# Which weights and values stay in SBUF between two rounds of a four-layer decode kernel, and where the others are put

## The chip, the cores and the metric

The kernel runs on one core of one Trainium2 chip. The metric is the device time of one execution in microseconds (us). The kernel before was run three times: 173.87, 174.04 and 174.45 us, a median of 174.04 us.

## What is computed

One token for each of four sequences goes through four residual layers: attention, gated unit, attention, gated unit. Both attentions use the same `wq`, `wo`, key and value caches, and both gated units the same `w_gate`, `w_up`, `w_down`.

```python
# x: 4 x 1 x 512, wq: 512 x 4096, wo: 4096 x 512; 32 query heads, 8 key/value heads of 128
def _A_ref(x, k_cache, v_cache, wq, wo):          # attention over the last W = 2048 positions
    q = (x @ wq).reshape(B, Sq, Hq, Dh).transpose(0, 2, 1, 3)
    k = jnp.repeat(k_cache[:, :, Sk - W:, :], rep, axis=1)
    v = jnp.repeat(v_cache[:, :, Sk - W:, :], rep, axis=1)
    p = softmax(einsum("bhqd,bhkd->bhqk", q, k) * Dh ** -0.5)
    return einsum("bhqk,bhkd->bhqd", p, v).transpose(0, 2, 1, 3).reshape(B, Sq, Hq * Dh) @ wo

def _B_ref(x, w_gate, w_up, w_down):              # 512 -> 1792 -> 512
    h = sigmoid(x @ w_gate) * (x @ w_up)
    return h @ w_down

x = x + _A_ref(layernorm(x), ...)
x = x + _B_ref(layernorm(x), ...)
x = x + _A_ref(layernorm(x), ...)
x = x + _B_ref(layernorm(x), ...)
```

All inputs are bf16. Keys and values of the window are 16 MiB each, `wq` and `wo` 4 MiB each, the three weights of the gated unit 1.75 MiB each.

## The kernel before: a plan of places, and one queue of loads

**Units.** SBUF places are counted in units: 256 bf16 columns on 128 partitions, 64 KiB. A head's keys or values (`V0_h` in the first attention, `V2_h` in the second) take 32 units, half of `wq` 32, one row block of `w_gate` or `w_up` 7 (`g0` to `g3`, `u0` to `u3`; two adjoining ones are loaded in one transfer of 14), and one of the 14 row blocks of `w_down` 2 (`d4` to `d6` is written `d4`, by its first block).

**Places.** `kt` holds all keys, transposed once in the first attention and read again in the second, where the values of later heads take the place of the keys that have been used. `wo_sb` (`ws` in the code) holds `wo`. `arena` (`ar`) has 75 units, `side` (`sx`) 31. `pt` holds softmax weights, `pb` the exponentials of the softmax, `qs` the queries. Between the attentions part of `wo_sb` (units 8 to 27) is copied to PSUM (`stash`, L1026, on VectorE at L1036) and copied back by ScalarE (L1031) at the start of the second attention, so that its place can take weights in between. The table `WHERE` (L430 and on) gives each tensor's place: buffer, first unit and length; `_1` or `_3` at the end of a name is the layer (first or second gated unit).

**What is kept.** Keys, `wo` and the second half of `wq` are read from HBM once. Of the values, the first attention leaves units 24 to 31 of head 0 in the arena (at 66) and units 19 to 31 of head 7 (at 23); `VKEEP` (L308) tells `load_v` (L471) to skip the load of these pieces in the second attention. Of the gated unit, `u01` and `g01` stay in the arena (`KEEPG`, L299; `load_g`, L1042). All else is loaded twice.

**Order.** All loads are issued by SyncE in one order, that of the program; a load waits, and with it all that come after it, until the instructions that read or wrote its place before are done. The other engines' instructions are ordered by a planner (`_schedule`) with fixed costs, and then run in that order, waiting on semaphores. The order of the loads from the end of the first attention on is: values of head 7 in two pieces, `u01`, `g01`, `g23`, `u23`, six pieces of `w_down`, the first half of `wq` in three pieces (`q01`), values of head 0 (24 units in four pieces) and head 1 (32 units in two), heads 2 to 7 into `kt`, `g23`, `u23`, four pieces of `w_down`.

**Instructions.** In the second attention a head goes through: scores (L763), their maximum and exponentials (L772 to L785), a turn (L791, L796), the weights (L821 on VectorE, L828 on ScalarE), the sums (L836), values (L921, or L863 and L879 where several heads' columns are packed), and `wo` (L961, L988). TensorE runs the score of a head two heads ahead of its values (`AHEAD`). The gated unit (`glu`, L1136) does `w_up` and `w_gate` at L1157 and `w_down` at L1233 in the first, at L1230 in the second. The queries of the second attention are made at L703, and the result of the second attention becomes the input of the last layer (`xn`) at L1071.

Of the kernel before, what the change touches and what calls it, by code (L numbers as in the profile page):

```python
# [268 lines left out]
def build(nc, A_x, A_k, A_v, A_wq, A_wo, B_wg, B_wu, B_wd, out):  # L269
# [4 lines left out]
    _, HKV, SK, DH = A_k.shape  # L274
# [24 lines left out]
    KEEPG = 4  # L299
# [8 lines left out]
    VKEEP = {0: 24, 7: 19}  # L308
# [30 lines left out]
    with es:  # L339
# [82 lines left out]
        G0 = MAIN - KEEPG * GU  # L422

# [7 lines left out]
        for n in range(HKV - 1):  # L431
            WHERE["V0_%d" % HEADS1[n]] = [ar(MAIN - UHEAD if n % 2 == 0 else 0, UHEAD)]
        WHERE["V0_%d" % (HKV - 1)] = [ar(0, 19), ar(23, 13)]
        WHERE["u01"], WHERE["g01"] = ar(52, 2 * GU), ar(38, 2 * GU)
        PT3 = ("kt", 187, 4)
        WHERE.update({
            "g23_1": ("ws", 8, 2 * GU), "u23_1": ar(0, 2 * GU),
            "d0_1": ar(14, 8), "d4_1": ("ws", 22, 6), "d7_1": ar(36, 2), "d8_1": ("qs", 0, 4), "d10_1": ("pb", 0, 4),
            "d12_1": ("pt", 4, 4),
            "q01": [("ws", 8, 10), ar(0, 14), ("ws", 18, 8)],  # L440
            "V2_0": [ar(14, 9), ar(36, 2), sx(0, 8), sx(8, 5), ar(66, 8)],
            "V2_1": [sx(13, NS - 13), ar(0, 14)],
            "V2_6": [("kt", 128, 16), ("kt", 144, 16)],
            "V2_7": [("kt", 160, 12), ("kt", 172, 7), ar(23, 13)],
            "g23_3": ar(0, 2 * GU), "u23_3": sx(0, 2 * GU),
            "d0_3": ar(14, 8), "d4_3": ("kt", 192, 8), "d8_3": ("kt", 200, 8), "d12_3": sx(14, 4),
# [595 lines left out]
        def load_g(L, nm, ktc, keep):  # L1042
            key = (nm, ktc // 2, 0 if keep or (nm, ktc // 2, 0) in gkeep else L)
            if key not in gkeep:
                s = WHERE["%s%d%d" % (nm, key[1] * 2, key[1] * 2 + 1) + ("_%d" % L if key[2] else "")]
                gkeep[key] = s
                dma("w%s%d_%d" % (nm, L, ktc), blk_ap(s), (wg_d if nm == "g" else wu_d)[:, key[1], :], w=blk_tok(s),
                    rate="bw_7k")
            s = gkeep[key]
            return (s[0], s[1] + ktc % 2 * GU, GU)  # L1050

        def load_d(L, fc0, fc1):
# [4 lines left out]
                w=blk_tok(s) + (("qs",), ("qs1",)) * (s[0] == "qs"), rate="bw_4k")  # L1057
# [78 lines left out]
        def glu(L, last_layer):  # L1136
# [10 lines left out]
            for nm, ktc in (("u", 0), ("u", 1), ("g", 0), ("g", 1), ("g", 2), ("g", 3), ("u", 2), ("u", 3)):  # L1147
                bank = GB if nm == "g" else UB
                keep = not last_layer and 2 * ktc + (nm == "u") < KEEPG
                s = load_g(L, nm, ktc, keep)  # L1150
# [64 lines left out]
            if not last_layer:  # L1215
                parts[1:] = [(4, 7), (7, 8), (8, 10), (10, 12), (12, 14)]
# [207 lines left out]
```

## Time and profile before

The profile is of another execution than the three timed ones.

| | us |
|---|---|
| timed runs | 173.87, 174.04, 174.45 |
| profiled execution, device time | 174.79 |
| its span, from the first to the last instruction | 173.0 |
| TensorE busy (matmul) | 136.2 |
| VectorE busy | 100.7 |
| ScalarE busy | 77.3 |
| HBM read | 68.62 MB, 397 GB/s over the span |
| mean granted TensorE clock | 0.822 |

The span runs from 0 to 173.0. The first attention takes it to about 105, the first gated unit to 119, the second attention to 162 and the last layer to the end. In the profile's slices a digit is the busy share in tenths of one fortieth of the span; in its timeline a row has a start, a duration, the engine, the line, what is written and read, a count of instructions, and in brackets the idle time of the engine before it with what ended that. A DMA row has the number of transfers, the size of each and the median time from issue to landing.

### The profile page before, as it was taken

What the parts mean: (1) busy time and instruction counts of PE and PEld (TensorE: products, weight loads), DVE (VectorE), ACT (ScalarE), POOL (GpSimd) and SP (SyncE); (2) the same over time, 40 slices, a digit from 0 to 9 for tenths busy, and PEclk for the clock granted to TensorE, in tenths of its full rate; (3) what the DMA queues carried; (4) which work ended last, traced back from release to release, by engine and by line L of the source; (5) the groups of instructions that cost most, each with busy time, mean ns of one, the idle gap of its engine ahead of it and who ended that gap; (6) DMA issues with size and microseconds to landing.
All of it is one profiled execution on the core that took longest, in us unless ns stands there. A gap on an engine that the chain in (4) does not pass through costs nothing.

```text
span 173.0 us, 4894 instructions
## 1 busy us (share of the span) xinstructions
PE 136.2 (79%) x2179; PEld 100.4 (58%) x2179; DVE 100.7 (58%) x252; ACT 77.3 (45%) x134; POOL 8.0 (5%) x19
## 2 busy tenths in 40 slices
PE   0395589899898779998979676657977989689883
PEld 0292388658466458565655366546625756458772
DVE  7535015886848675795797653113279877754450
ACT  2064207848576646566291230110767463554200
POOL 5200000000000000000000000202200000000020
PEclk9999756999999987999999755555569999956755
DMA  5999999999999999999999999999999999999960
GB/s 183 424 422 411 432 424 428 439 409 449 424 416 433 400 445 424 412 427 428 420 417 418 397 419 416 406 400 411 386 385 452 426 420 405 424 416 423 407 250 5
DMA packets 9361, 68.93 MB, mean 398 GB/s; under 512 B 1017, under 2 KB 1917, under 8 KB 6013
## 3 DMA queue, kind: packets, MB, share of 16 engines
q1 hardware_dynamic: 9332, 68.62, 95.7%
q8 instruction: 17, 0.28, 0.6%
q14 instruction: 4, 0.02, 0.0%
q10 hardware_dynamic: 8, 0.00, 0.0%
HBM read 68.62 MB, written 0.00 MB: 397 GB/s over the span
## 4 chain that ended last, share of the span: by engine, by line
DMA 65%; PE 23%; DVE 6%; ACT 2%; issue 2%; SPq 1%; DVEq 0%; ACTq 0%
DMA arena<-in_A_v_cache_dram 32%; DMA kt<-in_A_k_cache_dram 12%; DMA kt<-in_A_v_cache_dram 10%; DMA wo_sb<-in_B_w_down_dram 7%; PE ps L863 5%; PE ps L740 4%; DMA wo_sb<-in_A_wq_dram 4%; PE ps L763 3%; PE ps L1157 2%; PE ps L921 2%; SPq L464 1%; DVE pt L821 1%; PE ps L1230 1%; PE ps L836 1%; PE ps L988 1%
## 5 line engine op out<-in xcount | busy, mean ns | idle before, releaser
L750 ACT COPY kt<-ps 128x1024 bf16<-128x1024 bf16 x40 | 39.2, 1017 | 28.2 <-PE ps L740 28.0
L740 PE MATMUL ps<-ident_r,kt 128*128 128x128 bf16 x512 | 40.4, 238 | 5.1 <-DMA kt<-in_A_k_cache_dram 3.1
L740 PEld LDWEIGHTS ps<-ident_r,kt 128*128 128x128 bf16 x512 | 34.9, 109 | 11.8 <-issue 4.4
L750 DVE COPY kt<-ps 128x1024 bf16<-128x1024 bf16 x24 | 29.1, 1214 | 14.2 <-PE ps L740 14.0
L763 PE MATMUL ps<-kt,qs 128*32 128x512 bf16 x256 | 18.3, 413 | 1.2 <-ACT pb L785 1.2
L821 DVE TENSOR_TENSOR pt<-ps,ofbr 128x1024 bf16<-128x1024 f32 (+1 forms) x15 | 15.4, 1029 | 2.7 <-PE ps L796 2.7
L863 PE MATMUL ps<-arena,pt 128*64 128x512 bf16 (+1 forms) x128 | 13.1, 377 | 3.0 <-DMA arena<-in_A_v_cache_dram 3.0
L772 DVE TENSOR_REDUCE nmz<-ps 128x1 f32<-128x512 f32 x16 | 11.0, 688 | 5.9 <-PE ps L763 5.8
L791 DVE STREAM_TRANSPOSE pb<-pb 128x512 bf16<-128x512 bf16 x16 | 11.3, 704 | 4.2 <-ACT pb L785 4.1
L785 ACT ACTIVATE pb<-ps,nmz 128x512 bf16<-128x512 f32 x16 | 11.1, 692 | 5.8 <-DVE nmz L782 5.8
L828 ACT ACTIVATE pt<-ps,ofbr 128x96 bf16<-128x96 f32 x28 | 7.2, 342 | 7.8 <-PE ps L796 7.8
L863 PEld LDWEIGHTS ps<-arena,pt 128*64 128x64 bf16 (+1 forms) x128 | 5.9, 111 | 7.9 <-DMA arena<-in_A_v_cache_dram 4.0
L763 PEld LDWEIGHTS ps<-kt,qs 128*32 128x32 bf16 x256 | 5.8, 101 | 7.8 <-ACT pb L785 2.2
L872 ACT COPY arena<-ps 128x512 f32<-128x512 f32 (+1 forms) x7 | 3.9, 555 | 11.9 <-PE ps L863 11.7
L1031 ACT COPY wo_sb<-ps 128x1024 bf16<-128x1024 bf16 x5 | 5.0, 1011 | 9.1 <-PE ps L703 9.1
L836 PE MATMUL ps<-rowf,nmz 128*128 128x16 f32 x32 | 6.9, 292 | 2.7 <-DVE pt L821 2.5
L836 PEld LDWEIGHTS ps<-rowf,nmz 128*128 128x128 f32 x32 | 5.4, 212 | 5.8 <-DVE pt L821 4.2
L1157 PE MATMUL ps<-xn,arena 128*128 128x5 bf16 (+1 forms) x168 | 6.3, 172 | 2.2 <-DMA arena<-in_B_w_up_dram 1.1
L634 POOL TENSOR_TENSOR rs<-pt,rs 128x4 f32<-128x4 f32 x3 | 3.0, 1014 | 106.0 <-DVE pt L630 106.0
L879 PEld LDWEIGHTS ps<-arena 128*128 128x128 f32 x52 | 6.7, 201 | 2.1 <-ACT arena L872 1.6
L879 PE MATMUL ps<-arena 128*128 128x16 f32 x52 | 7.4, 273 | 0.6
L1157 PEld LDWEIGHTS ps<-xn,arena 128*128 128x128 bf16 x168 | 6.3, 118 | 2.5 <-DMA arena<-in_B_w_up_dram 1.2
(170 smaller groups left out, 162.9 us busy)
## 6 DMA issues: line engine op xcount, KB each, us to landing
kt<-in_A_k_cache_dram SPq DMA_DIRECT2D x8, 2048.0 KB, 24.6
arena<-in_A_v_cache_dram SPq DMA_DIRECT2D x7, 2048.0 KB, 20.2
kt<-in_A_v_cache_dram SPq DMA_DIRECT2D x3, 2048.0 KB, 14.9
wo_sb<-in_A_wo_dram SPq DMA_DIRECT2D x8, 512.0 KB, 25.1
kt<-in_A_v_cache_dram SPq DMA_DIRECT2D x4, 1024.0 KB, 19.3
kt<-in_A_wq_dram SPq DMA_DIRECT2D x1, 2048.0 KB, 11.7
side<-in_A_wq_dram SPq DMA_DIRECT2D x1, 1984.0 KB, 15.8
arena<-in_B_w_up_dram SPq DMA_DIRECT2D x2, 896.0 KB, 8.0
```

The costliest lines, as they stand in the source:

```text
L740: last = pe.transpose(bankb(bank)[:, (v * NB + q) * 128:(v * NB + q + 1) * 128], kt[:, c0:c0 + 128], ident_b[:, :])
L750: return (e.tensor_copy if ev == "vector" else e.copy)(to, fr)
L763: last = pe.matmul(ps[32 * b:32 * b + 32, sbk, 0:CB * 128], qs[:, q0:q0 + 32], blk_ap(kblk(h, b))[:, c * CB * 128:(c + 1) * CB * 128], sta ...
L772: lambda v: v.tensor_reduce(nmv, ps[:, sbk, 0:CB * 128], AXX, ALU.max, negate=True),
L785: o = a.activation(pbuf[:, :], ps[:, sbk, 0:CB * 128], ACTF.Exp, bias=gv, scale=1.0, accum_out=zv)
L791: P.op("vector", "ptr%d_%d" % (L, h), 650.0, lambda v: v.transpose(turned[:, :], pbuf[:, :]), r=[("pb", 0), ("pb", 1)], w=[("pb", 2), ("pb ...
L821: lambda v: v.tensor_tensor(pv4[:, 0:nj], spread(tbk, nj).unsqueeze(2).broadcast_to([128, nj, NB, REP]), ofb[:, :].unsqueeze(1).unsqueeze( ...
L828: last = a.mul(pv4[:, nj:NJ4, b, :], spread(MB, NJ4 - nj), ofb[:, b:b + 1])
L836: lambda pe: pe.matmul(ps[:, tbk, CB * NQ:CB * NQ + NR], zv.broadcast_to([128, 128]), rowf[:, :], start=True, stop=True),
L863: last = pe.matmul(ps[rows * g:rows * (g + 1), bank, 0:wide * 128].rearrange("p (c d) -> p c d", c=wide), ptv[:, w0:w0 + rows], v, start=( ...
L879: last = pe.matmul(ps[:, out[0], out[1]:out[1] + NR], part[:, c * 128:(c + 1) * 128], ey[wide][:, c * NR:(c + 1) * NR], start=(c == 0), st ...
L1157: last = pe.matmul(ps[:, bank, fc * wid:(fc + 1) * wid], cols[:, fc - g0, :], xn[:, ktc * (NB + 1):ktc * (NB + 1) + wid], start=(ktc == 0 ...
```

## The change

Other pieces stay, and nearly all transfers between the attentions get other places and a new order:

- **Values.** Head 0 keeps units 8 to 31 (24, at arena 50) instead of 24 to 31; head 7 keeps 17 to 31 (15, at arena 0) instead of 19 to 31.
- **Gate and up.** `u0`, `u1` and `g1` stay (21 units); `g0` is loaded again for the last layer, into `kt`.
- **First gated unit.** Loads come as `u01`, `g23`, `g01`, `u2`, `u3`; `u3` is in two pieces, in `pb` (4 units) and `qs` (3 units). TensorE takes the rows in the order `u0 u1 g2 g3 g0 g1 u2 u3`. `w_down` comes as `d4` (2 blocks), `d0` (4), `d8` (4), `d6` (2), `d12` (2) instead of `d0 d4 d7 d8 d10 d12`; `d0` and `d8` take the places of `g23` in `wo_sb`.
- **Queries of the second attention.** The first half of `wq` comes in four pieces of 10, 8, 10 and 4 units instead of 10, 14 and 8.
- **Second attention.** Before the loads into `kt` begin, 8 units of head 0 and 32 of head 1 are loaded.
- **Last layer.** `u01` and `g1` are there, then `g0`, `g23`, `u23` are loaded; its first `w_down` piece goes into `kt`.

The number of transfers is 63 for SyncE in both kernels. No arithmetic changes; sums over row blocks are taken in another order.

```diff
-    KEEPG = 4
+    KEPTG = {("u", 0), ("u", 1), ("g", 1)}
...
-    VKEEP = {0: 24, 7: 19}
+    VKEEP = {0: 8, 7: 17}
...
-        WHERE["V0_%d" % (HKV - 1)] = [ar(0, 19), ar(23, 13)]
-        WHERE["u01"], WHERE["g01"] = ar(52, 2 * GU), ar(38, 2 * GU)
+        WHERE["V0_%d" % (HKV - 1)] = [ar(15, 17), ar(0, 15)]
+        WHERE["u01"], WHERE["g01"] = ar(36, 2 * GU), ar(22, 2 * GU)
         PT3 = ("kt", 187, 4)
         WHERE.update({
-            "g23_1": ("ws", 8, 2 * GU), "u23_1": ar(0, 2 * GU),
-            "d0_1": ar(14, 8), "d4_1": ("ws", 22, 6), "d7_1": ar(36, 2), "d8_1": ("qs", 0, 4), "d10_1": ("pb", 0, 4),
-            "d12_1": ("pt", 4, 4),
-            "q01": [("ws", 8, 10), ar(0, 14), ("ws", 18, 8)],
-            "V2_0": [ar(14, 9), ar(36, 2), sx(0, 8), sx(8, 5), ar(66, 8)],
-            "V2_1": [sx(13, NS - 13), ar(0, 14)],
+            "g23_1": ("ws", 8, 2 * GU), "u2_1": ar(15, GU), "u3_1": ("pb", 0, 4), "u3_1b": ("qs", 0, 3),
+            "d4_1": ("ws", 24, 4), "d6_1": ("pt", 4, 4), "d0_1": ("ws", 8, 8), "d8_1": ("ws", 16, 8), "d12_1": ar(25, 4),
+            "q01": [ar(15, 10), ("ws", 8, 8), ("ws", 16, 10), ar(25, 4)],
+            "V2_0": [sx(0, 8), ar(50, 24)],
+            "V2_1": [sx(8, NS - 8), ar(15, 9)],
             "V2_6": [("kt", 128, 16), ("kt", 144, 16)],
-            "V2_7": [("kt", 160, 12), ("kt", 172, 7), ar(23, 13)],
-            "g23_3": ar(0, 2 * GU), "u23_3": sx(0, 2 * GU),
-            "d0_3": ar(14, 8), "d4_3": ("kt", 192, 8), "d8_3": ("kt", 200, 8), "d12_3": sx(14, 4),
+            "V2_7": [("kt", 160, 10), ("kt", 170, 7), ar(0, 15)],
+            "g0_3": ("kt", 0, GU), "g23_3": ar(15, 2 * GU), "u23_3": sx(0, 2 * GU),
+            "d0_3": ("kt", 8, 8), "d4_3": ("kt", 192, 8), "d8_3": ("kt", 200, 8), "d12_3": sx(14, 4),
         })
...
-            for nm, ktc in (("u", 0), ("u", 1), ("g", 0), ("g", 1), ("g", 2), ("g", 3), ("u", 2), ("u", 3)):
+            turn = [("u", 0), ("u", 1)] + [("g", a) for a in ((1, 0, 2, 3) if last_layer else (2, 3, 0, 1))] + [("u", 2), ("u", 3)]
+            for at, (nm, ktc) in enumerate(turn):
...
-                parts[1:] = [(4, 7), (7, 8), (8, 10), (10, 12), (12, 14)]
+                parts = [(4, 6), (0, 4), (8, 12), (6, 8), (12, 14)]
...
-        P.op("gpsimd", "qs_zero", 1200.0, lambda g: g.memset(qs[:], 0.0), w=[("qs",), ("qs1",)] + list(blk_tok(WHERE["d8_1"])))
+        P.op("gpsimd", "qs_zero", 1200.0, lambda g: g.memset(qs[:], 0.0), w=[("qs",), ("qs1",)] + list(blk_tok(WHERE["u3_1b"])))
```

The new `load_g` loads a row block by itself where `WHERE` names one, in two pieces if it names a second with a `b`, and otherwise the pair as before:

```python
        def load_g(L, nm, ktc):
            kept = (nm, ktc) in KEPTG
            name = "%s%d_%d" % (nm, ktc, L)
            if not kept and name in WHERE:
                got, f0 = [], 0
                for x in (name, name + "b"):
                    if x in WHERE:
                        s, c0 = WHERE[x], ktc % 2 * F + f0 * 128
                        dma("w" + x, blk_ap(s), (wg_d if nm == "g" else wu_d)[:, ktc // 2, c0:c0 + s[2] * UNIT], w=blk_tok(s) + qz(s),
                            rate="bw_4k")
                        got.append((s, f0))
                        f0 += 2 * s[2]
                return got
            key = "%s%d%d" % (nm, ktc // 2 * 2, ktc // 2 * 2 + 1) + ("" if ktc < 2 else "_%d" % L)
            s = WHERE[key]
            if key not in gkeep:
                gkeep[key] = s
                dma("w" + key, blk_ap(s), (wg_d if nm == "g" else wu_d)[:, ktc // 2, :], w=blk_tok(s), rate="bw_7k")
            return [((s[0], s[1] + ktc % 2 * GU, GU), 0)]
```

More of the change, by code (lines that the diff above doesn't have):

```diff
@@ L421, in build @@
         MAIN = WKEEP[2][0][1]
-        G0 = MAIN - KEEPG * GU
         def ar(u, n):
@@ L1040, in build, with qz @@
         gkeep = {}
-        def load_g(L, nm, ktc, keep):
-            key = (nm, ktc // 2, 0 if keep or (nm, ktc // 2, 0) in gkeep else L)
+        def qz(s):
+            return (("qs",), ("qs1",)) * (s[0] == "qs")
+        def load_g(L, nm, ktc):
[10 more added lines that the diff above has]
+                        f0 += 2 * s[2]
+                return got
+            key = "%s%d%d" % (nm, ktc // 2 * 2, ktc // 2 * 2 + 1) + ("" if ktc < 2 else "_%d" % L)
+            s = WHERE[key]
             if key not in gkeep:
-                s = WHERE["%s%d%d" % (nm, key[1] * 2, key[1] * 2 + 1) + ("_%d" % L if key[2] else "")]
                 gkeep[key] = s
[L1047 to L1050, printed above, removed]
+                dma("w" + key, blk_ap(s), (wg_d if nm == "g" else wu_d)[:, ktc // 2, :], w=blk_tok(s), rate="bw_7k")
+            return [((s[0], s[1] + ktc % 2 * GU, GU), 0)]
         def load_d(L, fc0, fc1):
@@ L1056, in load_d @@
             dma("wd%d_%d" % (L, fc0), blk_ap(s)[:, 0:(fc1 - fc0) * D], rows[:, (fc0 - g0) * D:(fc1 - g0) * D],
-                w=blk_tok(s) + (("qs",), ("qs1",)) * (s[0] == "qs"), rate="bw_4k")
+                w=blk_tok(s), rate="bw_4k")
             return s
@@ L1146, in glu, with e_g @@
             wid = NB if last_layer else NB + 1
-            for nm, ktc in (("u", 0), ("u", 1), ("g", 0), ("g", 1), ("g", 2), ("g", 3), ("u", 2), ("u", 3)):
+            turn = [("u", 0), ("u", 1)] + [("g", a) for a in ((1, 0, 2, 3) if last_layer else (2, 3, 0, 1))] + [("u", 2), ("u", 3)]
+            for at, (nm, ktc) in enumerate(turn):
                 bank = GB if nm == "g" else UB
-                keep = not last_layer and 2 * ktc + (nm == "u") < KEEPG
-                s = load_g(L, nm, ktc, keep)
-                def e_g(pe, ktc=ktc, s=s, bank=bank):
+                first, end = ktc == turn[0 if nm == "u" else 2][1], ktc == turn[-1 if nm == "u" else 5][1]
+                got = load_g(L, nm, ktc)
+                def e_g(pe, ktc=ktc, got=got, bank=bank, first=first, end=end):
                     last = None
@@ L1155, in e_g @@
                         g0, gn = WD[fc // 4]
-                        cols = blk_ap(s)[:, g0 * 128:(g0 + gn) * 128].rearrange("p (m j) -> p j m", j=gn)
+                        s, f0 = [x for x in got if x[1] <= fc][-1]
+                        cols = blk_ap(s)[:, (g0 - f0) * 128:(g0 - f0 + gn) * 128].rearrange("p (m j) -> p j m", j=gn)
                         last = pe.matmul(ps[:, bank, fc * wid:(fc + 1) * wid],
@@ L1159, in e_g @@
                                          xn[:, ktc * (NB + 1):ktc * (NB + 1) + wid],
-                                         start=(ktc == 0 and fc == 0), stop=(ktc == NC - 1),
-                                         skip_group_check=True)
+                                         start=(first and fc == 0), stop=end, skip_group_check=True)
                     return last
                 prev = [P.op("tensor", "glu_%s%d_%d" % (nm, L, ktc), 36.0 * NFC, e_g,
-                             r=list(blk_tok(s)) + [("xn",)], w=[("psg", bank, ktc)], banks=(bank,), order=prev)]
+                             r=[t for s, _ in got for t in blk_tok(s)] + [("xn",)], w=[("psg", bank, ktc)], banks=(bank,), order=prev)]
                 toks[nm].append(("psg", bank, ktc))
@@ L1233, in e_d @@
                                 last = pe.matmul(ps[:, YB, c * NB:(c + 1) * NB], wd, hf,
-                                                 start=(fc == 0 and c == 0), stop=(fc == NFC - 1),
+                                                 start=(fc == parts[0][0] and c == 0), stop=(fc == parts[-1][1] - 1),
                                                  skip_group_check=True)
```

## The prediction

> **What bounds the kernel now.** I read the slices of the profile first, then the DMA rows, then what TensorE waited for in the second attention, then its timeline.
>
> The slices (a digit per fortieth of the span, 4.3 us each):
>
> ```profile
> PEclk9999756999999987999999755555569999956755
> DMA  5999999999999999999999999999999999999960
> GB/s 183 424 422 411 432 424 428 439 409 449 424 416 433 400 445 424 412 427 428 420 417 418 397 419 416 406 400 411 386 385 452 426 420 405 424 416 423 407 250 5
> DMA packets 9361, 68.93 MB, mean 398 GB/s; under 512 B 1017, under 2 KB 1917, under 8 KB 6013
> ```
>
> The DMA engines are full from the first slice to the 38th, the passage between the attentions (slices 23 to 29) included. So fewer bytes are worth time, if the queue stays full and what follows the last loads can move up as well. Second, who waits at the end. The waits of TensorE between 126 and 163 us (total, times, longest):
>
> ```profile
> PE ps L863 <- DMA kt<-in_A_v_cache_dram: 1.6, 3, 0.9
> PE ps L836 <- DVE pt L821: 1.4, 2, 0.9
> PE ps L763 <- ACT pb L785: 1.2, 2, 0.7
> ```
>
> and its timeline there and in the last layer:
>
> ```profile
> 142.57 1.06 PE L863 MATMUL ps<-kt,pt 128*32 128x256 bf16 x32 [0.36 <-DMA kt<-in_A_v_cache_dram]
> ...
> 147.49 1.06 PE L863 MATMUL ps<-kt,pt 128*32 128x256 bf16 x32 [0.35 <-DMA kt<-in_A_v_cache_dram]
> ...
> 149.99 0.62 PE L863 MATMUL ps<-kt,pt 128*32 128x256 bf16 x16 [0.90 <-DMA kt<-in_A_v_cache_dram]
> ...
> 162.47 0.23 PE L1157 MATMUL ps<-xn,arena 128*128 128x4 bf16 x2 [0.28 <-DVE xn L1071]
> ...
> 170.03 0.53 PE L1230 MATMUL ps<-side,pt 128*25 128x128 bf16 x8
> ```
>
> The reader is to see that TensorE is nearly as long as the loads: of the 36 us from 126 to 162 it stands still for about 6, and for values only 0.36 + 0.35 + 0.90 = 1.6 us. After 162.47 it never waits for a load; the last load, 256 KB of `w_down` issued at 150.28 with 18.8 us to landing, is there at 169.05, 1.0 us before its matmuls at 170.03. So a byte saved is worth its transfer time to the loads, but only what TensorE has been waiting to the time.
>
> **Part 1: bytes.** Kept before: 8 + 13 units of values and 28 of gate and up, 49. After: 24 + 15 and 21, 60. So 11 units of 64 KiB, 0.72 MB, are not loaded. Heads 3 and 4 of the values, 32 units each, reach TensorE at 142.57 and 147.49, 4.92 us for 32 units: 0.154 us a unit. 11 units are 1.7 us. Where they are missing matters: heads 0 and 1 load 40 units instead of 56, so heads 2 to 6 land 16 x 0.154 = 2.5 us earlier; head 7 loads 17 instead of 19, so 18 units or 2.8 us for its last piece; `g0` (7) comes again, which leaves 1.7 us for everything after it. The last load should land at 169.05 - 1.7 = 167.35.
>
> **Part 2: the passage between the attentions.** 84 units stand between the values of head 7 and `wq` in both kernels (56 of gate and up, 28 of `w_down`), and 32 of `wq` behind, in the same number of transfers. The added waits are all on SyncE's queue, and behind each waits every later load. What a late issue costs needs the lead. The nearest row for a transfer into an empty queue is the output: 0.7 us of issue and 1.0 us of waiting for it, 1.7 us in all. Two rows of the passage:
>
> ```profile
> wo_sb<-in_A_wq_dram SPq DMA_DIRECT2D x1, 512.0 KB, 6.9
> side<-in_A_v_cache_dram SPq DMA_DIRECT2D x1, 512.0 KB, 6.7
> ```
>
> 512 KB need 8 x 0.16 + 1.7 = 3.0 us in an empty queue and took 6.7 at the least: the queue held nearly 4 us of work at its thinnest. A load that has to land at time T with u units does no harm if it is issued by T - 0.16 u - 1.7. Now each added wait, with landings from the rows of TensorE:
>
> ```profile
> 115.05 0.59 PE L1233 MATMUL ps<-pt,arena 128*128 128x4 bf16 x16 [1.54 <-DMA arena<-in_B_w_down_dram]
> ...
> 118.42 0.38 PE L1233 MATMUL ps<-pt 128*128 128x4 bf16 x8 [0.28 <-DMA pt<-in_B_w_down_dram]
> ```
>
> The first 8 units of `w_down` land at 115.0, all 28 at 118.4: 0.17 us a unit.
> - `u01` now covers the sums' place (arena 36, 37) and the identity at 40, which head 0's L879 reads until 100.4; before it was issued at 98.89. It landed 6.9 us later, at 105.8, so it may be issued until 105.8 - 2.2 - 1.7 = 101.9. Spare 1.5 us, cost 0.
> - `g01` waits for head 7's first piece, as `u23` did (issued 103.39); it has the place of `g23` in the queue, landing 110.2. Cost 0. `u3` waits for the turn of `pb` (L1014, done at 104.1): cost 0, `pb` lay in this queue before too.
> - `d0` goes where `g23` lay, so it waits for `g2`, `g3`. `g23` comes 14 units sooner, at 108.0, and TensorE is free for it after `u0`, `u1` at about 109.0 (`xn` first used at 107.39; 14 matmuls 0.5 to 0.6 us): issue at 110.1. As 12 of 28 units it has to land at 118.4 - 16 x 0.17 = 115.7, so by 112.7. Spare 2.6.
> - `wq`'s second piece goes where `d0` lay: 115.7 + 0.6 for 16 matmuls, issue at 116.3; it has to land 18 units after 118.4, at 121.3, so by 118.3. Spare 2.0. The third waits for `d8` (20 of 28 units, 117.0 + 0.6): 117.6 against 119.6. Spare 2.0. The fourth waits for `d12`, 118.8 against 121: spare 2.
> - The values of head 2 into `kt` still wait for the first scores, issued at 125.92. They landed 11.5 us later, at 137.5; now they are wanted at 135.0, so by 135.0 - 5.0 - 1.7 = 128.3. Spare 2.4 where it was 4.9. This is the stall that would be late next.
>
> Smaller rows (`u3` in 4 and 3 units) are about as many as go (pieces of 2 units), and 256 KB pieces follow each other at 0.7 us against 4 x 0.154: 0.1 us at most, either way; I take 0. The chain to the queries keeps its ends: `u3` lands at the 56th unit as `u23` did (112.4), `w_down` at 118.4, `wq` at 123.4; ScalarE's copies back start some 0.5 us later and are still ahead of the scores that need their banks. So I start the second attention at the same time.
>
> **Part 3: the second attention and the end.** With values 2.5 us earlier the three waits of 1.6 us go. VectorE is busy for 21.5 of the 26.5 us from 125.9 to 152.4, so it has room for this. The planner changes the order a little (head 4's scores come ahead of the turn of head 2's weights, the last head's scores later), so some of the 1.4 us at L836 and 1.2 us at L763 may grow; bounds 0 and the 1.6 won, I take 0.1. From `xn` to the end nothing waits for loads, before or after: `g23` and `u23` land 1.7 us earlier, the input 1.5. The bound by the loads is 170.03 - 167.35 = 2.7 us.
>
> **Sum.** 174.79 for the profiled execution, less 1.6, plus 0.1: 173.3 (span 171.5). The profiled execution stands 0.75 over the median of the runs; the same change on the median gives 174.04 - 1.5 = **172.5**.
>
> **Rivals.**
> 1. *More, up to the bound of the loads.* The clock:
>
> ```profile
> 148.87:152.28 3.41, 1.96 (x30) 1.46 (x30) 1.90 (x7) 1.52 (x6) 0.00 (x0) 1.00 1.02 425
> 152.28:159.10 6.82, 6.37 (x128) 4.84 (x129) 3.05 (x8) 3.19 (x9) 0.00 (x0) 0.50 1.00 411
> ```
>
> TensorE was busy for 1.96 of 3.41 us (first columns: window, length, TensorE), the 0.9 us wait among the rest, and then had half the clock for 6.8 us. At half the clock 16 matmuls of L863 took 1.07 for 0.62, L879 1.03 for 0.56, two groups of L988 0.60 for 0.39, L836 0.59 for 0.39: with the rest about 1.7 us. If the wait goes and the clock stays, 1.6 + 1.7 exceeds the bound of 2.7: 171.3. Against it: other short waits remain, and from 128.4 to 131.8 TensorE was as idle and kept its clock. The Trainium skill, "TensorE: Matmul & The Clock Gate", section "What's actually happening", says that the clock is halved after a free-running window of about 3.4 us with too little work; 6.8 us is two of these, and by that rule this rival would be the forecast.
> 2. *No change.* The loads are hidden: the waits for values turn into waits for VectorE, ScalarE or a reordered TensorE, and the start of the last layer stays at 162. For it: VectorE is busy for 3.33 of 3.42 us from 145.45 to 148.87. Against: it has idle time on both sides. 1.6 us won, 1.1 to 1.9 given back: 173.5 to 174.4, say 174.0.
> 3. *Slower: the ring of places runs dry.* `d0` waits for `g3`, `wq`'s second piece for `d0`, head 2's values for the queries from `wq`. If `d0`'s matmuls end more than 2.0 us after 116.3, every us more delays `wq`, the queries and so all of the second attention by one. To lose 0.7 net it takes 2.0 + 1.6 + 0.7 = 4.3 us: 174.7. Only a landing far off its place in the queue does that; against it speak the spares above.
> 4. *The load isn't skipped.* `load_v` skips where the kept piece begins at the unit in `VKEEP` (8, 17), which the new pieces do. I give this nothing of its own.
>
> **How the numbers follow.** Forecast (172.0 to 173.4) 0.58; rival 1 (171.0 to 172.0) 0.18; rival 2 0.15; rival 3 0.09. About 0.3% or 0.5 us is what a measurement of this kernel can tell from no change. Faster by that: 0.58 + 0.18 = 0.76; the same: rival 2, 0.15; slower 0.09. The range takes in the two neighbours, from the 171.3 of rival 1 to 174.1 in rival 2; it leaves out some 0.09 + 0.08.
>
> **What would show it.** HBM read 67.9 MB instead of 68.62. In the slices DMA stays at 9 through the passage. SyncE issues `wq`'s second piece near 116.3, head 2's values near 126. TensorE's waits for values of 1.6 us are gone, L1071 near 160.7 instead of 162.23, the last load at 167.3. Wrong would be a hole in DMA between 112 and 130 (rival 3), new waits of 1 us for L821 or L785 with L1071 at 162 (rival 2), or a full clock from 150 to 159 (rival 1).

## The result, and the profile after

The kernel after is slower: 175.17 us (median of 19 runs, 174.49 to 176.61) against 174.12 (19 runs, 173.38 to 174.6) for the kernel before in the same series. The ratio is 1.0068, with a 95% interval of 1.0052 to 1.0083. The forecast was 172.5, with a range of 171.3 to 174.1: a gain of 1.5 us was predicted (from 174.04), and a loss of 1.05 came.

The profiled execution of the kernel after took 176.61 us (span 174.8), the slowest of its runs, so it overstates the loss. A time read from a profile below is that of one execution. The slices after, to be held against those of before:

```profile
PEclk9999656999999999999999655555558699975555
DMA  5999999999999999999999999999989999999960
GB/s 181 420 436 426 420 424 420 431 411 446 420 424 427 404 432 435 415 430 412 435 425 402 396 332 406 387 352 353 358 346 410 429 424 411 420 417 416 410 262 6
HBM read 67.90 MB, written 0.00 MB: 389 GB/s over the span
```

The bytes are those that were predicted (67.90 MB). But the rate, which before was 385 to 452 GB/s in the passage (slices 23 to 32), is 332 in slice 24 and 346 to 358 in slices 27 to 30, and slice 30 has a DMA digit of 8. The windows of the passage in the kernel after, then in the kernel before (columns: window, length, busy TensorE, weight loads, VectorE, ScalarE, GpSimd, clock, DMA share, GB/s):

```profile
100.50:104.90 4.40, 3.38 (x58) 2.69 (x59) 2.41 (x6) 1.68 (x2) 0.00 (x0) 0.50 0.90 331
113.00:118.00 5.00, 1.96 (x53) 1.68 (x51) 0.51 (x3) 1.48 (x2) 0.97 (x1) 0.50 0.93 349
118.00:123.00 5.00, 4.23 (x127) 3.90 (x125) 1.94 (x11) 0.00 (x0) 0.50 (x2) 0.50 0.94 361
...
128.00:132.00 4.00, 3.22 (x30) 0.75 (x22) 2.56 (x9) 1.79 (x4) 0.00 (x0) 0.56 0.93 360
```

```profile
100.50:104.90 4.40, 3.52 (x82) 2.83 (x82) 1.94 (x7) 1.87 (x2) 0.00 (x0) 0.50 1.02 420
113.00:118.00 5.00, 2.34 (x64) 2.01 (x61) 0.51 (x3) 0.21 (x1) 0.42 (x1) 0.50 1.04 403
118.00:123.00 5.00, 4.34 (x131) 4.06 (x127) 1.94 (x11) 0.72 (x1) 1.75 (x3) 0.50 1.02 404
...
128.00:132.00 4.00, 2.29 (x32) 1.08 (x36) 3.62 (x9) 2.93 (x9) 0.00 (x0) 0.95 1.06 441
```

In the 14.4 us of the first three windows the kernel before moved 420 x 4.4 + 403 x 5 + 404 x 5 = 5883 KB, the kernel after 5006: 0.88 MB less, where the change saves 0.72 MB in all. The fourth window, in the first heads of the second attention, adds 0.32 MB. From 100 to 140 us the kernel after moved 15.02 MB, the kernel before 16.44; from there to the last loads it stays about as far behind. So it had lost 1.42 MB of transfers by then, twice what it saves, and its last load lands later (171.00 us) than before (169.05). A rate below that of before isn't by itself a loss of time: f4, the kernel before with its code shifted (below), moved 329 GB/s from 118 to 123 us and took no measurably longer. What TensorE waits for in the kernel after from the second attention's first scores to the end (total, times, longest; the first five rows):

```profile
PE ps L761 <- ACT pb L783: 1.2, 2, 0.7
PE ps L794 <- DVE pb L789: 1.0, 3, 0.4
PE ps L834 <- DVE pt L819: 0.9, 1, 0.9
PE ps L1170 <- issue: 0.9, 1, 0.9
PE ps L1242 <- issue: 0.5, 1, 0.5
```

The 1.6 us of waits for values (L863 before, L861 now) are gone, as predicted. New are 1.0 for the turn (L794) and 1.46 of "issue", where it was 0.76. The passage itself, in TensorE's timeline:

```profile
116.55 0.58 PE L1245 MATMUL ps<-pt,wo_sb 128*128 128x4 bf16 x16 [1.00 <-DMA wo_sb<-in_B_w_down_dram]
117.83 0.59 PE L1245 MATMUL ps<-pt,wo_sb 128*128 128x4 bf16 x16 [0.69 <-DMA wo_sb<-in_B_w_down_dram]
...
124.10 0.70 PE L701 MATMUL ps<-xn,wo_sb 128*128 128x4 bf16 x20 [0.68 <-DMA wo_sb<-in_A_wq_dram]
124.72 0.37 PE L701 MATMUL ps<-xn,arena 128*128 128x4 bf16 x8
125.57 2.75 PE L761 MATMUL ps<-kt,qs 128*32 128x512 bf16 x24 [0.48 <-DVE pt L714]
```

The last instruction that makes the input of the second attention (L560) starts at 119.59, the first scores at 125.57: 5.98 us. Before it was 118.83 (L562) and 123.98: 5.15.

A measure that recurs below: the distance from that input to the first scores (the passage), from the first scores to the first values in `kt`, from there to the input of the last layer (L1071 before, L1082 after), and from there to the end. Each row is one execution. The second and third distance trade against each other (g4, a form of the kernel before, has 16.83 and 21.30 in its profile), so a single one of them says little.

| profile | passage | to values in kt | to last layer | to the end | last load lands |
|---|---|---|---|---|---|
| before | 5.15 | 15.02 | 23.23 | 10.82 | 169.05 |
| after | 5.98 | 16.17 | 21.52 | 11.51 | 171.00 |
| after, g23 ahead (e3) | 5.95 | 15.49 | 21.29 | 11.54 | 169.70 |
| after, code shifted (f3) | 6.07 | 16.71 | 21.54 | 10.11 | 169.84 |

### The profile page after: what moved, and what is told of

Same layout as the page of the kernel before. It is cut to its first block, busy times and chain, and to the rows that moved or that the text cites. A ratio compares the mean times of both kernels' runs of the same rounds, so it can differ in the third digit from the quotient of the medians.

```text
span 174.8 us, 4895 instructions
## 1 busy us (share of the span) xinstructions
PE 135.9 (78%) x2179; PEld 99.3 (57%) x2179; DVE 100.8 (58%) x252; ACT 77.2 (44%) x134; POOL 8.0 (5%) x19
## 3 DMA queue, kind: packets, MB, share of 16 engines
q1 hardware_dynamic: 9332, 67.90, 94.7%
HBM read 67.90 MB, written 0.00 MB: 389 GB/s over the span
## 4 chain that ended last, share of the span: by engine, by line
DMA 62%; PE 25%; DVE 5%; issue 2%; ACT 2%; SPq 2%; DVEq 0%; ACTq 0%
DMA arena<-in_A_v_cache_dram 32%; DMA kt<-in_A_k_cache_dram 12%; DMA kt<-in_A_v_cache_dram 11%; PE ps L761 5%; PE ps L861 4%; PE ps L738 4%; DMA wo_sb<-in_B_w_down_dram 4%; PE ps L1170 3%; DMA wo_sb<-in_A_wq_dram 3%; PE ps L919 3%; SPq L462 2%; PE ps L1242 1%; ACT pb L783 1%; PE ps L834 1%; DVE nmz L770 1%
## 5 line engine op out<-in xcount | busy, mean ns | idle before, releaser
L738 PE MATMUL ps<-ident_r,kt 128*128 128x128 bf16 x512 | 39.1, 233 | 5.6 <-DMA kt<-in_A_k_cache_dram 3.5
L738 PEld LDWEIGHTS ps<-ident_r,kt 128*128 128x128 bf16 x512 | 33.4, 107 | 12.7 <-issue 4.0
L761 PE MATMUL ps<-kt,qs 128*32 128x512 bf16 x256 | 19.6, 438 | 1.7 <-ACT pb L783 1.2
L861 PE MATMUL ps<-arena,pt 128*64 128x512 bf16 (+1 forms) x128 | 13.4, 391 | 4.1 <-DMA arena<-in_A_v_cache_dram 4.1
L861 PEld LDWEIGHTS ps<-arena,pt 128*64 128x64 bf16 (+1 forms) x128 | 6.0, 117 | 9.4 <-DMA arena<-in_A_v_cache_dram 5.3
L1170 PE MATMUL ps<-xn,arena 128*128 128x5 bf16 (+1 forms) x140 | 5.7, 173 | 2.6 <-issue 0.9
L1170 PEld LDWEIGHTS ps<-xn,arena 128*128 128x128 bf16 x140 | 5.5, 118 | 3.0 <-issue 1.6
## 6 DMA issues: line engine op xcount, KB each, us to landing
kt<-in_A_v_cache_dram SPq DMA_DIRECT2D x3, 2048.0 KB, 14.4
```

The costliest lines, as they stand in the source:

```text
L738: last = pe.transpose(bankb(bank)[:, (v * NB + q) * 128:(v * NB + q + 1) * 128], kt[:, c0:c0 + 128], ident_b[:, :])
L761: last = pe.matmul(ps[32 * b:32 * b + 32, sbk, 0:CB * 128], qs[:, q0:q0 + 32], blk_ap(kblk(h, b))[:, c * CB * 128:(c + 1) * CB * 128], sta ...
L861: last = pe.matmul(ps[rows * g:rows * (g + 1), bank, 0:wide * 128].rearrange("p (c d) -> p c d", c=wide), ptv[:, w0:w0 + rows], v, start=( ...
L1170: last = pe.matmul(ps[:, bank, fc * wid:(fc + 1) * wid], cols[:, fc - g0, :], xn[:, ktc * (NB + 1):ktc * (NB + 1) + wid], start=(first and ...
```

## The experiments

Every kernel was timed against the kernel before on the same chip in the same series; ratios are to that, with 95% intervals. The kernel after stands at 1.0068.

**First series: are bytes worth time, and which wait hurts?** e1 and e4 leave loads out of the kernel before, so that stale data is read in their place; e2 loads again what the change keeps.

```diff
# e1, e4: before, in load_v
-                if L == 2 and VKEEP.get(h) == u0:
+                if L == 2 and (VKEEP.get(h) == u0 or h == 0 and u0 in (0, 9, 19)):                  # e1, 16 units
+                if L == 2 and (VKEEP.get(h) == u0 or h in (3, 4) or h == 5 and u0 == 0):            # e4, 80 units
# e2: after
-    VKEEP = {0: 8, 7: 17}
-            "V2_0": [sx(0, 8), ar(50, 24)],
+    VKEEP = {0: 24, 7: 17}
+            "V2_0": [sx(0, 8), ar(50, 16), ar(66, 8)],
# e3: after, in glu ahead of the loop over the rows
+            if not last_layer:
+                load_g(L, "g", 2)
```

> The kernel before, with 16 of the 24 units of head 0's values not loaded in the second attention (three pieces are left out and stale data is read in their place); every place and every other wait stays. So 1.05 MB less is moved, and 40 units instead of 56 stand before the loads into kt, as in the changed kernel. Theory R (the ring of places: in the changed kernel loads are issued too late, the queue runs dry in the passage between the attentions, and this costs more than the bytes bring): here the places are those of before, so the bytes pay: faster by 1 to 1.6 us. Theory T (TensorE and its clock: the second attention and the last layer cannot move up, and the reordered instructions cost): within 0.4 us of before, or slower.

Measured: 174.41 us (12 runs), ratio 1.0010 (0.9986 to 1.0033): no gain from 16 units, which by the prediction's 0.154 us a unit are 2.46 us of loads. In the profile the last load lands at 168.21 instead of 169.05, so 0.84 of the 2.46 arrive; from 100 to 140 us 15.74 MB were moved instead of 16.44. The first load into `kt` is issued when the first scores are done, at 125.75 here and at 125.92 before. What stands ahead of it in the queue is shorter by 16 units, and most of that turns into a thinner queue (303 GB/s from 123 to 128 us, before 370). TensorE's waits for values become one of 1.6 us, and it gets 0.99 of "issue" in the last layer.

> The changed kernel, with 16 of head 0's 24 kept units loaded again in the second attention into the place where they lie (nothing waits for that place). Bytes are then those of before plus 5 units less; the places and waits of the passage are those of the changed kernel. Theory R: the added load comes while the engines stand still for want of issued loads, so it is partly or wholly free: 0 to 1 us over the changed kernel, and clearly over before by 1 to 2 us, since the places alone carry the loss. Theory T: the loads aren't the bound, so 0 over the changed kernel within 0.4, or under it if the order of TensorE returns to that of before.

Measured: 176.95 (6 runs), 1.0159 (1.0122 to 1.0196): in the new places 16 units more cost 0.9%, 1.6 us. That is more than either theory allowed (up to 1 us, and within 0.4). So the two experiments aren't mirror images: 16 units taken out of the kernel before bring nothing, and 16 units put back into the kernel after cost most of their 2.46 us. Why they cost so much there was not shown.

> The changed kernel with the load of g2 and g3 issued ahead of that of u0 and u1. Its place in wo_sb is free at about 98, that of u0 and u1 only at 101.3, so the queue gets 14 units 3 us sooner; the rest stays. Theory R: the hole in DMA at 100 to 104 us (289 to 360 GB/s instead of 410) closes; 0.3 to 0.9 us faster than the changed kernel. Theory T: no change within 0.3 us, although the hole closes.

Measured: 175.33 (12 runs), 1.0062 (1.0038 to 1.0085), as the kernel after. The hole at 100 to 104 us is closed, the passage is 5.95: that hole isn't the loss.

> The kernel before, with the values of heads 3 and 4 and half of head 5 not loaded in the second attention (stale data is read in their place), 80 units or some 12 us of loads left out. TensorE then never waits for values. This measures how far the second attention and the last layer can move up at all. Theory R: loads pace this stage, TensorE has room of 2 us or more: 172 or less. Theory T: TensorE is the bound, 172.5 to 174.

Measured: 171.62 (6 runs), 0.9852 (0.9823 to 0.9881). 80 units, 12.3 us of loads by the same figure, bring 2.5 us. The last load lands at 158.88 and the span ends at 170.02, so loads no longer set the end: 2.5 us is all that fewer loads can bring here.

**Second series: the passage, and the stalls named "issue".** f1 puts two pieces of `wq` where head 0's kept values lie, which it spoils; f2 puts one into `pb`; f3 and f4 repeat four transposes at the start 17 times, in the kernel after and before.

```diff
# f1, f2: after
-            "q01": [ar(15, 10), ("ws", 8, 8), ("ws", 16, 10), ar(25, 4)],
+            "q01": [ar(15, 10), ar(50, 8), ar(58, 10), ar(25, 4)],              # f1
+            "q01": [ar(15, 10), ("pb", 0, 4), ("ws", 8, 8), ("ws", 16, 10)],    # f2
# f3, f4: after, before
-            for c in range(NC):
+            for c in list(range(NC)) * 17:
```

> The changed kernel with the second and third piece of wq's first half put into the arena at 50 to 67, where nothing has to be waited for, instead of into the places of w_down's pieces in wo_sb. Bytes, transfers and their order stay. (These units held kept values of head 0, which are overwritten, so head 0's values are wrong for 18 units.) Theory R (late issue of wq): from the input of the second attention to its first scores 5.1 us instead of 6.0, as in the kernel before, and 0.8 us faster than the changed kernel. Theory T (TensorE, its clock and its code): the scores start earlier, but the time stays within 0.3 us.

Measured: 174.76 (12 runs), 1.0036 (1.0015 to 1.0057); passage 5.67. A part of the delay is the late issue of `wq`. The time lies between what the two theories gave.

> The changed kernel with wq's first half in the pieces arena 10 units, pb 4, wo_sb 8, wo_sb 10, instead of 10, 8, 10 and 4 in the arena at 25; pb is free as soon as u3 has been used. So each wait for w_down has 4 units or 0.6 us more of queue ahead of it. Theory R: half to all of the 0.85 us between the input and the first scores comes back, 0.4 to 0.8 us faster than the changed kernel. Theory T: within 0.3 us.

Measured: 175.41 (11 runs), 1.0061 (1.0036 to 1.0085); passage 6.08. The last piece, which still waits for `w_down`'s matmuls, has 10 units now, and all queries wait for it.

> The changed kernel with the first transposes of x (4 matmuls) made 17 times, 64 matmuls more at 2 to 6 us, where TensorE waits for keys anyway. All later instructions of TensorE lie 64 matmuls, half a block of code of 128, further on. Theory C (the waits called issue, 0.92 us at the start of the last layer and 0.54 us before the last matmuls, are for code): they leave these two places, and the time moves by up to 0.7 us either way. Without C: the waits stay at the same instructions and the time within 0.3 us.

Measured: 174.96 (12 runs), 1.0045 (1.0026 to 1.0064). The "issue" of 0.92 and 0.54 us in the last layer is gone from its places; one of 0.31 stands at another, and one of 0.70 has come up in the second attention (147.73). So they belong to the place of an instruction in the code, not to its work.

> The kernel before with the same 64 matmuls more at the start. Theory C: the waits called issue (0.24 us at L1157 and 0.52 us at L1230) move to other instructions, the time by up to 0.7 us. Without C: same time within 0.3 us and the waits where they were.

Measured: 174.27 (12 runs), 1.0025 (0.9999 to 1.0051). Its two stalls of 0.24 and 0.52 became one of 0.66: no gain. With the code shifted alike, the kernel after stands at 1.0045 and the kernel before at 1.0025; the intervals overlap.

The longest chain of the kernel after shows where such a stall lies (start, length, what):

```profile
163.50 0.23 PE ps L1170 x2
163.72 0.92 issue
164.64 0.99 PE ps L1170 x26
...
169.79 0.48 PE ps L1242 x9
170.27 0.54 issue
170.80 1.49 PE ps L1242 x47
```

In the DMA records there are 17 packets of 16 KB of instructions to 2179 matmuls, one for every 128. One of them is moved from 162.09 to 163.11, and TensorE goes on at 164.64, 1.53 us after its end. So it is throughout: in the 20 profiles TensorE has 38 stalls named "issue" of 0.17 us or more after 100 us, and each ends 1.2 to 1.6 us after the end of such a packet. TensorE waits for its code there. That the full queue of loads makes the code late is likely, but no run here shows it.

**Third series: the cut of `wq`.** Before, 24 units complete the queries of half of the heads; after, a piece ends at the 28th only.

```diff
# g1, g2, g3: after (g3 with g23 ahead as e3, and the transposes of f3)
-            "q01": [ar(15, 10), ("ws", 8, 8), ("ws", 16, 10), ar(25, 4)],
+            "q01": [ar(15, 10), ("ws", 8, 8), ("ws", 16, 6), ("ws", 22, 4), ar(25, 4)],   # g1
+            "q01": [ar(15, 10), ar(50, 14), ar(64, 8)],                                   # g2
+            "q01": [ar(15, 10), ("pb", 0, 4), ("ws", 8, 8), ("ws", 16, 2), ("ws", 18, 8)],  # g3
# g4: before
-            "q01": [("ws", 8, 10), ar(0, 14), ("ws", 18, 8)],
+            "q01": [ar(0, 10), ("ws", 8, 8), ("ws", 16, 10), ar(10, 4)],
```

> The kernel after, with wq's first half in pieces of 10, 8, 6, 4 and 4 units instead of 10, 8, 10 and 4, all in places it used already: a piece ends at the 24th unit, as before, where the queries of the first half of the heads are complete. The last two pieces still wait for w_down's matmuls. The planner now puts 16 of the first score's matmuls ahead of the last queries'. Theory P (0.85 us of the loss is the passage from the second attention's input to its first scores: about 0.5 for the cut, which makes all queries wait for the 28th unit, and 0.35 for the late issues, and it passes through to the end): input to first scores 5.4 to 5.5 us instead of 6.0, time 0.4 to 0.5 us less than after, 174.7. Rival H (an earlier start of the scores is worth nothing, since the values into kt and the clock set the pace): the same passage, time 175.1 to 175.3. Rival Q (the cut doesn't matter, the landing of the whole does): passage 6.0, time 175.2.

Measured: 175.11 (11 runs), 1.0057 (1.0033 to 1.0081); passage 4.94. The passage is mended, by 1.0 us, and the time is not.

> The kernel after, with wq's first half in the three pieces of before (10, 14, 8 units), in places that no w_down matmul holds: so no late issue and a piece that ends at the 24th unit. The places are those of head 0's kept values, 22 units of which are overwritten and then used, so head 0's output is wrong; the work and the loads are as many. Theory P: input to first scores 5.1 to 5.2 us, time 0.8 to 0.9 less than after, 174.3. Rival H: the passage is 5.15 and the time 175.0 or more, because TensorE then waits for values into kt or for its clock. If the passage stays over 5.5, something else of the new places makes it long.

Measured: 175.05 (6 runs), 1.0062 (1.0040 to 1.0085); passage 5.33. The same: rival H, not P.

> The kernel after with all that could be mended without a wrong place: wq in pieces of 10, 4, 8, 2 and 8 units (the second in pb, so that only 14 units wait for w_down's matmuls, and a piece ends at the 24th), g23 of the first gated unit issued ahead of u01, and 64 more matmuls at the start, which shift TensorE's code fetches. Theory P: passage 5.3, 0.7 less; the code shift 0.2; the earlier g23 nothing: 174.3, no better than the kernel before (174.15). Rival H: 174.9. A bound: were the clock's loss in the first heads bound to the late start, it would go too, 173.4.

Measured: 174.18 (12 runs), 1.0009 (0.9987 to 1.0031); passage 5.16. With these parts mended the loss is gone, about the sum that P gave (174.3); but g1 and g2 forbid to lay it to the passage alone. The stalls for code haven't all gone: one of 0.69 us stands in the second attention, one of 0.17 in the last layer. What ends last is now something else. Its longest chain:

```profile
149.68 18.95 DMA kt<-in_B_w_down_dram
168.63 0.04 issue
168.68 0.61 PE ps L1244 x16
169.29 0.01 issue
169.30 0.43 PE ps L1244 x8
```

TensorE waits for the third piece of `w_down`. The last load lands at 169.25, later than before (169.05), though 11 units less were loaded.

> The kernel before, with wq's first half in pieces of 10, 8, 10 and 4 units as in the kernel after, instead of 10, 14 and 8, in the same places of arena and wo_sb taken in another order; the third piece still waits for w_down's fifth to seventh block only, as the last did, so nothing is issued later. Theory P: all queries are complete at the 28th unit only: input to first scores 5.6 to 5.7 us instead of 5.15, time 0.4 to 0.5 more than before, 174.6. Rival H: the same passage, time 174.2. Rival Q: passage 5.15, time 174.2.

Measured: 174.12 (12 runs, 173.29 to 175.57), 1.0013 (0.9984 to 1.0041); passage 5.43. The cut by itself lengthens the passage by 0.28 (the code shift of f4, which touches no load, by 0.41) and costs no time that can be measured. P falls as a theory of the whole.

**Fourth series: the clock.** In all ten profiles with changed places or cut up to here the clock was at half for 2 us or more between 131 and 138 us (in f2 and f3 it had not risen yet); in none of the four others. For each window of the clock of 3.41 us in all 20 profiles, the columns of the matmuls that start in it were summed, each weighted by the share of the array that it uses (a score counts a quarter). Of 73 full-clock windows that were followed by half the clock, 70 have a sum below 2740; of 512 that kept it, 8. The bound was chosen on these same profiles. The filling matmuls of h1 below, 512 columns each, start 0.22 us apart at full clock, so some 8000 columns fit into a window, and the bound is near a third. The first heads stand at it: 2848 in the profile before (kept), 2336 in g2 (lost). Their windows (columns as above):

```profile
128.38:131.80 3.42, 2.00 (x28) 0.88 (x32) 3.04 (x8) 2.55 (x7) 0.00 (x0) 1.00 1.06 442
131.80:135.21 3.41, 3.35 (x92) 2.51 (x88) 3.21 (x10) 1.70 (x6) 0.00 (x0) 1.00 1.02 432
```

```profile
127.91:131.32 3.41, 1.66 (x20) 0.74 (x20) 3.13 (x8) 3.02 (x8) 0.00 (x0) 1.00 1.03 422
131.32:134.73 3.41, 3.08 (x56) 1.71 (x57) 2.59 (x8) 1.23 (x7) 0.00 (x0) 0.50 1.02 437
```

Up to 131 us the two kernels run the same instructions at the same distances from the first scores. The windows lie differently to them: one ends 7.8 us after the first scores and takes in the start of the third score, the other at 7.1. The Trainium skill, "TensorE: Matmul & The Clock Gate", section "What's actually happening", has the window free-running, so that this differs from run to run; the traces agree: in before, e1 and e4, which run the same instructions up to there, the clock rises 4.40, 2.82 and 5.53 us after the first scores. The test adds full-array work in a gap, in four kernels:

```diff
             turns.append(scores(2, n, h, SB2[n % 2], TB2[n % 2]))
+            if n == 0:
+                def e_fill(pe, k=4):
+                    for _ in range(k):
+                        last = pe.matmul(ps[:, 5, :], perm[:, :], ident_r[:, :], start=True, stop=True, skip_group_check=True)
+                    return last
+                P.op("tensor", "fill", 880.0, e_fill, r=[("pspt", TB2[0]), ("perm",), ("ident_b",)],
+                     w=[("fill",)], banks=(5,))
```

> The kernel after with four matmuls of 512 columns on the whole array (their result is not used) on TensorE behind the turn of head 0's weights in the second attention, where it stands still for 0.92 us. They add 2048 array-columns to every window of the clock that starts 2.6 to 5.3 us after the first scores. Theory W (the sum of a window decides, and the lost window costs about 0.85 us in most executions): no half clock between 131 and 138 us once it was full, first scores to head 2's values 15.4 us instead of 16.2, time 174.3 to 174.6. Rival X (the clock falls for another reason, or its fall is hidden behind the loads): half clock as before, or no gain: 175.1 to 175.4, the four matmuls delaying the first weights by up to 0.2.

Measured: 175.03 (12 runs), 1.0048 (1.0025 to 1.0070). The clock stays full from 130.4 to 154.3, and first scores to values in `kt` falls to 14.71; the time hardly moves. Its profile shows one thing that can have taken the gain: the four matmuls shift the code fetch by four, from just behind the last layer's first matmuls into the ones just ahead of it, where the stall is longer:

```profile
161.00 0.54 PE L893 MATMUL ps<-onb,wo_sb 128*128 128x4 bf16 x14 [0.29 <-DVE onb L930]
163.02 0.22 PE L893 MATMUL ps<-onb,wo_sb 128*128 128x4 bf16 x2 [1.48 <-issue]
```

> The mended form of the kernel after (wq in pieces of 10, 4, 8, 2 and 8 with the second in pb, g23 ahead of u01, 64 more matmuls at the start), with the four filling matmuls. Theory W: 0.6 to 0.9 less than without them, 173.3 to 173.6, faster than the kernel before. Rival X: 174.2 to 174.4.

Measured: 174.50 (12 runs), 1.0004 (0.9983 to 1.0024): a miss for W's time, the clock again full (127.4 to 154.7). It waits 0.60 us for `w_down` at the end instead of 0.32; the last load lands at 169.63.

> The kernel before with the four filling matmuls. Its windows are under the bound only where they start 3.0 to 4.0 us after the first scores, about three in ten if the phase is free; it kept its clock in all profiles so far. Theory W: no half clock between 131 and 138, and 0 to 0.3 less, 173.9 to 174.2. Rival X: up to 0.2 more, 174.2 to 174.4.

Measured: 174.04 (12 runs), 0.9990 (0.9968 to 1.0013). Clock full from 127.0 to 154.3, no "issue" in the last layer; no gain that can be told.

> The kernel before with 64 more matmuls at the start and the four filling matmuls: the same treatment as the mended form of the kernel after has had, apart from the places and the cut. Theory W: 173.9 to 174.2, and the mended after is 0.4 to 0.8 faster than this, which is then what the change is worth once its own stalls are gone. Rival X: the same as the mended after within 0.2.

Measured: 174.91 (12 runs), 1.0023 (1.0001 to 1.0045). Clock full, but a stall of 1.00 in the last layer. W's time is missed here too. None of the four lost the clock, but only h1 and h2 test the rule: the kernel before kept its clock without the filling, and so does k1 below, a form of the kernel after. A full clock there is worth no time that could be measured, and beyond h1 it didn't shorten the way from the first scores to the values in `kt` by much: 15.36 us in h2 for 15.50 in g3, 15.01 in h3 for 15.03 before, 15.82 in h4 for 15.36 in f4. The last loads of these four land at 169.21 to 169.74, no sooner than before. h2 and h4 have had the same treatment apart from the places, the cut and the order of `g23`, and h2 is 0.4 us faster, as W had it; the intervals of their ratios, 1.0004 and 1.0023, overlap.

**Fifth series: the queue.** The loads of the passage get places for which no matmul of `w_down` has to end first. For that the kept values of heads 0 and 7 are partly overwritten, and then used.

```diff
# k2: after; k1: g3
-            ... "d0_1": ("ws", 8, 8), "d8_1": ("ws", 16, 8), ...
-            "V2_0": [sx(0, 8), ar(50, 24)],
+            ... "d0_1": ar(50, 8), "d8_1": ar(58, 8), ...
+            "q01": [ar(15, 10), ("ws", 8, 14), ar(66, 8)],
+            "V2_0": [ar(0, 8), ar(50, 24)],
```

> The mended form of the kernel after (g23 ahead of u01, 64 more matmuls at the start) with places for w_down's second and third piece, wq's last and head 0's first values that nobody uses at that time, and wq in 10, 14 and 8 units: no load of the passage waits for a matmul of w_down. The places are those of kept values of heads 0 and 7, which are overwritten and then used, so the values of these heads are partly wrong; work and bytes are as many. Theory Q (the saved bytes are lost as holes in the queue of loads, which the late issues make): the last load lands at 167.6 to 168.3 us instead of 169.25, and the time is 173.2 to 173.7, less than that of the kernel before. Rival R (the loads run slower for another reason, such as the cuts or the code fetches): last load at 169 or later, 174.0 to 174.4.

Measured: 173.98 (12 runs), 0.9982 (0.9957 to 1.0007), its profile 173.25 with the last load at 168.37. The load lands 0.9 sooner than in g3 and misses Q's 168.3 by little; the median misses Q's 173.7 by 0.3 and R's 174.0 by 0.02. It is the fastest form of the change, and not told from the kernel before.

> The kernel after with the same free places and wq in 10, 14 and 8 units, and nothing else changed: g23 comes behind u01, and TensorE's code is fetched where it was, so its two stalls in the last layer (0.9 and 0.5 us) stay. Head 0's and 7's values are partly wrong. Theory Q: last load 168.0 to 168.7 (instead of 169.4 to 169.8; the hole at 101 to 104 us stays), passage 5.2 us instead of 6.0, time 174.0 to 174.5 instead of 175.17. Rival R: last load at 169.3 or later, time 174.9 to 175.2.

Measured: 174.54 (12 runs), 1.0019 (0.9995 to 1.0043); passage 5.16. The time is above Q's range by 0.04 and far from R's. Against Q: the last load lands at 169.84 in its profile, where R had it (169.3 or later); this was its slowest run (175.23). The stalls of 0.91 and 0.25 are there, as foreseen.

## Why the prediction was wrong

1. **"A byte saved is worth its transfer time to the loads" failed first.** Even in the kernel before 16 units bring 0.10% the wrong way (-0.14 to +0.33), and the last load gains 0.84 us of 2.46. The queue is refilled at moments that the computation sets: the values of head 1 when the kept `wq` rows have been read (issued 120.99 before, 121.75 after), the first load into `kt` after the first scores (125.92, 127.51). 16 of the saved units stood just ahead of these moments, so their absence made the queue thinner there, not the loads earlier. `g0`, which is loaded again, stands behind them, where the queue is full; that it costs in full follows from this, but was not tested by itself. "The last load should land at 167.35": it landed at 171.0 in the profile after, and at 169.1 to 169.8 in nine of its forms (e3, f1 to f3, g1 to g3, h1, h2).
2. **Part 2, "cost 0", failed by its lead.** A load was to do no harm if issued by T - 0.16 u - 1.7. The loads that had to wait for a place were issued inside this limit, and landed late (us, in the profile after):

   | load | issued | limit | landed | had to land | from issue to landing | by the formula |
   |---|---|---|---|---|---|---|
   | `d0`, 8 units | 110.82 | 112.7 | 116.51 | 115.7 | 5.7 | 3.0 |
   | `wq`, second piece, 8 units | 117.17 | 118.3 | 121.90 | 121.3 | 4.7 | 3.0 |
   | `wq`, third piece, 10 units | 118.45 | 119.6 | 124.06 | 122.9 | 5.6 | 3.3 |
   | values of head 2, 32 units | 127.51 | 128.3 | 138.56 | 135.0 | 11.1 | 6.7 |

   Behind `d0` the last `w_down` piece landed at 119.13 instead of 118.4, so the input came 0.76 later; for `wq`'s third piece TensorE waited 0.68 us. The limit took the queue for one empty pipe with one end. But loads ahead are still in it (head 1's last piece landed at 132.16, 4.65 us after head 2's values were issued), and the 16 parts of one load land apart: 1.6 us for `wq`'s second piece, 2.8 for head 2's values, 3.4 for the last `w_down` piece in the profile before (115.01 to 118.37). Giving these loads free places (k2) brings the ratio from 1.0068 to 1.0019: some 0.8 us of the 1.05 lie here, by the two intervals 0.3 to 1.4. k2 has the cut of `wq` of before too. `wq` alone does not bring it (f1 1.0036, g1 1.0057, g2 1.0062); which of `d0`, `d8` and head 0's first values adds the rest was not separated.
3. **"The chain to the queries keeps its ends" failed.** The passage is 5.95 to 6.08 in after, e2, e3, f2 and f3 (6.51 in h1), 5.10 to 5.17 in before, e1, e4 and h3 (5.56 and 5.79 with the code shifted, f4 and h4). A part is the late `wq`, another the cut, which the prediction didn't price. It also counted as many transfers of `w_gate`, `w_up`, `w_down` and `wq` as before; there are 15 instead of 13. The passage mended by itself (g1, g2) is worth nothing that could be measured.
4. **Part 3 was right on the waits and wrong on what follows.** The 1.6 us at L863 went, and from the first values in `kt` to the last layer the profile after is 1.7 us shorter. But this stretch starts 2.7 us later in it (0.76 before the input, 0.83 in the passage, 1.15 in the first heads, which spend longer at half the clock), so that L1082 comes at 163.26 instead of the 160.7 forecast for it; and "from `xn` to the end nothing waits" overlooked two things. The "issue" of the last layer, 0.76 before, is 1.05 to 1.50 in five of eight forms of the change with unshifted code (after, e3, f1, g2, k2; 0 to 0.55 in e2, f2, g1). And when that is mended the last load is the next bound: g3, h2 and h3 end 2.9 to 3.1 us after it.
5. **Rival 3 was the right side, for nearly its reason.** The ring of places did run dry, but it didn't take the 4.3 us that the rival asked for: `wq`'s second piece was only 0.9 later than forecast. Rival 1 didn't come: its sign was a full clock from 150 to 159, and in the profile after the clock fell at 155.40 and stayed at half to the end (before: half from 152.28 to 159.10, full to 162.52). What h1 to h4 show is about another stretch, the first heads: a full clock there brought no time that could be measured.

What stays open: how the 1.05 us divide exactly, and how much of them is owed to the places and how much to where the code happens to be cut (with the code shifted alike f3 and f4 stand at 1.0045 and 1.0025, h2 and h4 at 1.0004 and 1.0023). It also stays open why 16 units cost 1.6 us in e2 where 16 units bring nothing in e1. Single runs of one kernel spread over 1 to 2 us, the parts are 0.2 to 0.8 each, and they don't add (the passage alone brings 0, all parts together 1.0). No form that leaves the kept values alone beats the kernel before: g3 (1.0009) and h2 (1.0004) equal it.

## What to carry to other kernels

A byte saved isn't worth its transfer time as a matter of course. Look, before counting bytes, for the loads whose issue waits for a computation: 16 units taken out ahead of the last of them were worth nothing here (e1), 80 units behind it 2.5 us (e4). It isn't a rule without exception: 16 units put back ahead of it cost 1.6 us (e2). Price a place that must first be set free by a measured landing of a load into a thin queue (here 4.7 to 5.7 us for 8 to 10 units), not by the mean rate and the latency of an empty queue. Where several bounds lie within 1% of each other, a mend of one shows nothing, and only mends in combination, and stalls counted in several profiles, tell them apart.

## What the hardware showed unexpectedly

- TensorE's code comes through the DMA engines that move the loads, 16 KB for 128 matmuls in 0.9 to 1.4 us a packet. Where TensorE stood still for 0.2 to 1.5 us at such a boundary, it went on 1.2 to 1.6 us after the packet's end. Shifting the code by 4 or 64 matmuls moved the stall and changed its length, from 0 to 1.48.
- The clock of TensorE follows here the weighted columns of a window, about a third of what fits, not its busy share: TensorE busy for 2.00 of 3.42 us (128.38 to 131.80) kept the clock in the profile before (sum 2848), for 1.98 of 3.41 (131.51 to 134.92) lost it in the one after (sum 2688).
